# Keeping the FFN activations token-major and taking the F-major copies from transposing DMA loads (SSM block with gated FFN, forward and backward)

## Chip, cores, metric

One core of one Trainium2 chip. The metric is the device time of one execution in microseconds (us), median of several runs. The kernel before took 2763.79 us (3 runs, 2761.97 to 2766.11). "Times in the trace" count from the start of the span.

## The reference

L = 2048 tokens, D = 576 channels, N = 128 states, F = 4608 hidden FFN columns, all bf16. The kernel returns the output and the gradients of all parameters.

```python
xn = _layernorm(x)
s  = ssm(xn, A, B, C, log_dt, Dskip)       # long convolution by FFT
gate = einsum("bsd,df->bsf", xn, w1)
up   = einsum("bsd,df->bsf", xn, w3)
h    = silu(gate) * up
g    = silu(einsum("bsf,fd->bsd", h, w2))
out  = x + s * g                           # and the vjp of all of it with grad_out
```

## The kernel before

The FFN's activations live in DRAM as F-major tiles, [F, tokens]. The backward pass of the FFN has two stages. The *weight stage* goes over 18 groups of 256 F columns; the weight gradients contract over tokens and so need token-major h, gu and gg, which PE makes by transposing F-major tiles through PSUM.

```python
def pe_transpose(self, dst, src):                      # 16 transposes of 128x128
    for g in range(LT // 8):
        pt = self.ps_tr.tile([P, 8, P], BF16, name="ptr6")
        for k in range(8):
            nc.tensor.transpose(pt[:, k, :], src[:, t * P:(t + 1) * P], self.ident_bf[:])
        # evicted by VectorE (g even) or ScalarE (g odd)
...
    nc.vector.memset(go_oT[rem:P, DT - 1, :], 0.0)     # 5th chunk padded to 128 rows
...
    for hh in range(NH):                               # hidden gradient gh, F-major
        ph = ps_h.tile([P, HL], FP32, name="ph")       # HL = 512 tokens
        for c in range(DT):                            # 5 chunks, all of 128 rows
            nc.tensor.matmul(ph[...], lhsT=w2T[:, c, :], rhs=go_oT[:, c, ...],
                             start=(c == 0), stop=(c == DT - 1))
        nc.scalar.copy(out=gh[:, hh * HL:(hh + 1) * HL], in_=ph[:])
```

The *input stage* loads F-major gg and gu for 256 tokens at a time, transposes w1 and w3 by 72 DMA loads, and runs the last GEMM (tile `px`).

Of the kernel before, what the change touches and what calls it, by code (L numbers as in the profile page):

```python
# [11 lines left out]
ALU = mybir.AluOpType  # L12
# [46 lines left out]
class K:  # L59
# [567 lines left out]
    def ffn_scratch(self):  # L627
        cfg = self.cfg
        D, DT, L, LT, FT = cfg.D, cfg.DT, cfg.L, cfg.LT, cfg.FT
        self.TC4 = 256  # L630
        self.G_dram = self.dram.tile([FT, P, L], BF16, name="G_dram")
        self.U_dram = self.dram.tile([FT, P, L], BF16, name="U_dram")
        self.H_dram = self.dram.tile([L // self.TC4, P, FT, self.TC4], BF16, name="H_dram")
        self.GS_dram = self.dram.tile([P, LT, D], BF16, name="GS_dram")
        self.GO_dram = self.dram.tile([P, LT, D], BF16, name="GO_dram")
        self.GOT_dram = self.dram.tile([P, DT, L], BF16, name="GOT_dram")

    def ffn_hidden(self, wp, gup, ps, T0, TA):
# [3 lines left out]
        GRP = 4  # L642
        HL = 1024
        nfull = D // P
        rem = D - nfull * P
        assert FT % GRP == 0 and rem == 64
        xnT = self.xnT
        for fi in range(FT):
            self.at(T0 + TA * fi)
            f0 = fi * P  # L650
            fl = fi % GRP
            if fl == 0:
                wm = {}
                for w in ("B_w1", "B_w3"):
                    wm[w] = wp.tile([P, nfull, GRP * P], BF16, name="wm" + w)
                    nc.sync.dma_start(out=wm[w][:], in_=aps[w][0:nfull * P, f0:f0 + GRP * P].rearrange(
                        "(c p) f -> p c f", p=P))
                wt = wp.tile([P, GRP * P], BF16, name="wtail")
                nc.sync.dma_start(out=wt[0:rem, :], in_=aps["B_w1"][nfull * P:D, f0:f0 + GRP * P])
                nc.sync.dma_start(out=wt[rem:P, :], in_=aps["B_w3"][nfull * P:D, f0:f0 + GRP * P])  # L660
            cs = slice(fl * P, (fl + 1) * P)
            for hh in range(L // HL):
                g_t = gup.tile([P, HL], BF16, name="g_t")
                u_t = gup.tile([P, HL], BF16, name="u_t")
                s_t = gup.tile([P, HL], BF16, name="s_t")
                h_t = gup.tile([P, HL], BF16, name="h_t")
                for q in range(HL // 512):
                    qs = slice(q * 512, (q + 1) * 512)
                    t0 = hh * HL + q * 512
                    pg = ps.tile([P, 512], FP32, name="pg")  # L670
                    pu = ps.tile([P, 512], FP32, name="pu")
                    for (w, pt) in (("B_w1", pg), ("B_w3", pu)):
                        for c in range(nfull):
                            nc.tensor.matmul(pt[:], lhsT=wm[w][:, c, cs], rhs=xnT[:, c, t0:t0 + 512], start=(c == 0),  # L674
                                             stop=False)
                    nc.tensor.matmul(pg[:], lhsT=wt[0:rem, cs], rhs=xnT[0:rem, nfull, t0:t0 + 512], start=False, stop=True)
                    nc.tensor.matmul(pu[:], lhsT=wt[rem:P, cs], rhs=xnT[rem:P, nfull, t0:t0 + 512], start=False, stop=True)
                    nc.scalar.activation(out=s_t[:, qs], in_=pg[:], func=ACT.Silu)
                    if q % 2 == 0:
                        nc.vector.tensor_copy(out=g_t[:, qs], in_=pg[:])  # L680
                    else:
                        nc.scalar.copy(out=g_t[:, qs], in_=pg[:])  # L682
                    nc.scalar.copy(out=u_t[:, qs], in_=pu[:])  # L683
                nc.vector.tensor_tensor(out=h_t[:], in0=s_t[:], in1=u_t[:], op=ALU.mult)
                nch = HL // self.TC4
                nc.sync.dma_start(out=self.H_dram[hh * nch:(hh + 1) * nch, :, fi, :].rearrange("c p l -> p c l"),
                                  in_=h_t[:].rearrange("p (c l) -> p c l", l=self.TC4))
                nc.gpsimd.dma_start(out=self.G_dram[fi, :, hh * HL:(hh + 1) * HL], in_=g_t[:])
                nc.gpsimd.dma_start(out=self.U_dram[fi, :, hh * HL:(hh + 1) * HL], in_=u_t[:])

    def ffn_output(self, T0, TB):
# [3 lines left out]
        TC = self.TC4  # L695
# [5 lines left out]
        with self.tc.tile_pool(name="o_w", bufs=1) as wpool, \  # L701
                self.tc.tile_pool(name="o_h", bufs=3) as hp, \
# [10 lines left out]
            for i in range(LT):  # L713
                self.at(T0 + TB * i)
                k = i % (TC // P)
                if k == 0:
                    hc = hp.tile([P, FT, TC], BF16, name="hc")
                    nc.sync.dma_start(out=hc[:], in_=self.H_dram[i // (TC // P)])
# [7 lines left out]
                for fi in range(FT):  # L726
                    for pi_, (po, pw) in enumerate(pieces):
                        nc.tensor.matmul(po_[:, pi_, 0:pw], lhsT=hc[:, fi, k * P:(k + 1) * P],  # L728
# [247 lines left out]
    def phase6_ffn_bwd(self):  # L976
        nc, cfg = self.nc, self.cfg
        L, FT = cfg.L, cfg.FT
        self.TC6 = 256
        self.GG_dram = self.dram.tile([L // self.TC6, P, FT, self.TC6], BF16, name="GG_dram")  # L980
        self.GU_dram = self.dram.tile([L // self.TC6, P, FT, self.TC6], BF16, name="GU_dram")
        self.phase6_weights()
        self.phase6_inputs()
# [4 lines left out]
    def pe_transpose(self, dst, src):  # L988
        nc, LT = self.nc, self.cfg.LT
        for g in range(LT // 8):  # L990
            pt = self.ps_tr.tile([P, 8, P], BF16, name="ptr6")
            for k in range(8):
                t = g * 8 + k
                nc.tensor.transpose(pt[:, k, :], src[:, t * P:(t + 1) * P], self.ident_bf[:])  # L994
            if g % 2 == 0:
                nc.vector.tensor_copy(out=dst[:, g * 8:(g + 1) * 8, :], in_=pt[:])
            else:
                nc.scalar.copy(out=dst[:, g * 8:(g + 1) * 8, :], in_=pt[:])

    def phase6_weights(self):  # L1000
        nc, cfg = self.nc, self.cfg
        D, DT, L, LT, F, FT = cfg.D, cfg.DT, cfg.L, cfg.LT, cfg.F, cfg.FT
        aps = self.aps
        GRP = 2
        NGRP = FT // GRP
        HL = 512
        NH = L // HL
        pieces = self.dpieces()
        nfull = D // P
        rem = D - nfull * P  # L1010
        assert FT % GRP == 0 and rem == 64
        with self.tc.tile_pool(name="e_big", bufs=1) as big, \
                self.tc.tile_pool(name="e_w", bufs=2) as wp, \
                self.tc.tile_pool(name="e_in", bufs=2) as inp, \
                self.tc.tile_pool(name="e_el", bufs=2) as elp, \
                self.tc.tile_pool(name="e_t", bufs=2) as tp, \
                self.tc.tile_pool(name="e_hn", bufs=3) as hnp, \
                self.tc.tile_pool(name="e_nat", bufs=2) as natp, \
                self.tc.tile_pool(name="e_gw", bufs=2) as gwp, \
                self.tc.tile_pool(name="e_ps_h", bufs=2, space=bass.MemoryType.PSUM) as ps_h, \  # L1020
                self.tc.tile_pool(name="e_ps_tr", bufs=2, space=bass.MemoryType.PSUM) as self.ps_tr, \
                self.tc.tile_pool(name="e_ps_w2", bufs=1, space=bass.MemoryType.PSUM) as ps_w2, \
                self.tc.tile_pool(name="e_ps_gw", bufs=2, space=bass.MemoryType.PSUM) as ps_gw:
            go_o = big.tile([P, LT, D], BF16, name="go_o6")
            go_oT = big.tile([P, DT, L], BF16, name="go_oT6")
            nc.vector.memset(go_oT[rem:P, DT - 1, :], 0.0)
# [3 lines left out]
            for gi in range(NGRP + 1):  # L1030
                if gi < NGRP:
                    tiles = self.phase6_elementwise(gi, GRP, wp, inp, elp, tp, hnp, natp, ps_h, go_oT)
                if gi > 0:
                    self.phase6_weight_grads(gi - 1, GRP, prev, go_o, gwp, ps_w2, ps_gw)
                prev = tiles

    def phase6_elementwise(self, gi, GRP, wp, inp, elp, tp, hnp, natp, ps_h, go_oT):
        nc, cfg = self.nc, self.cfg
        D, DT, L, LT, FT = cfg.D, cfg.DT, cfg.L, cfg.LT, cfg.FT
        aps = self.aps  # L1040
        HL = 512
        NH = L // HL
        gg_n = natp.tile([P, LT, GRP * P], BF16, name="gg_n")
        gu_n = natp.tile([P, LT, GRP * P], BF16, name="gu_n")
        gates, ups, silus, dsls, h_ns = [], [], [], [], []
        for fl in range(GRP):
            fi = gi * GRP + fl
            gate = inp.tile([P, L], BF16, name="gate6")
            nc.gpsimd.dma_start(out=gate[:], in_=self.G_dram[fi])
            gates.append(gate)  # L1050
            silu = elp.tile([P, L], BF16, name="silu6")
            nc.scalar.activation(out=silu[:], in_=gate[:], func=ACT.Silu)
            silus.append(silu)
        for fl in range(GRP):
            dsl = elp.tile([P, L], BF16, name="dsl6")
            self.dsilu(elp, dsl, gates[fl], silus[fl])
            dsls.append(dsl)
        for fl in range(GRP):
            fi = gi * GRP + fl
            up = inp.tile([P, L], BF16, name="up6")  # L1060
            nc.gpsimd.dma_start(out=up[:], in_=self.U_dram[fi])
            hT = elp.tile([P, L], BF16, name="hT6")
# [240 lines left out]
```

## Time and profile before

| stage of the kernel before | from, to (us) | what it is bound by |
|---|---|---|
| SSM forward and first FFN GEMMs | 252, 919 | a chain through PE, DVE and ACT |
| FFN output GEMM (`po`) | 937, 1103 | PE |
| SSM parameter gradients (`pT`) | 1396, 1577 | transposing loads |
| weight stage (`ph`, `pgw`) | 1639, 2391.5 | PE, 41.4 us a group |
| input stage (`px`) | 2391.5, 2759.7 | transposing loads, then PE |

The columns of a timeline are start, length, engine, line, operation, operand, count.

### The profile page before, as it was taken

The numbers are of one execution on the slowest core, as the hardware profiler recorded it, in microseconds if no ns is written. First come the engines' busy times: TensorE is split into PE (matmuls) and PEld (weight loads), VectorE is DVE, ScalarE is ACT, GpSimd is POOL, SyncE is SP. The second block draws the span as 40 slices with busy tenths as digits, with TensorE's granted clock in tenths as the row PEclk, the third lists the DMA queues.
The fourth block names the chain that finished last, engine by engine and source line by source line (L and its number), as shares of the span: only waits on it lengthen the run. The fifth ranks groups of instructions, "written<-read, shape, count | busy, mean of one in ns | idle before, by whom it ended". The sixth has DMA issues, their size and how long they took to land.

```text
span 2759.7 us, 39491 instructions
## 1 busy us (share of the span) xinstructions
PE 2061.2 (75%) x15803; PEld 1342.9 (49%) x15894; DVE 1473.6 (53%) x2361; ACT 1083.3 (39%) x1381; POOL 409.0 (15%) x655
## 2 busy tenths in 40 slices
PE   1797777777899699435343329899999999639999
PEld 0332233223355377324233316676776777527777
DVE  7313767667688355697988964443433444102222
ACT  1357777776755211202000027565565565000000
POOL 1001333333211211000000002222222221100000
PEclk9556787787899899768655559999999999869999
DMA  2245666666764774222299946455454443475441
GB/s 73 91 185 212 238 237 215 222 221 239 260 212 159 261 244 130 78 87 73 64 237 237 230 112 184 143 141 133 144 143 130 142 135 105 96 200 201 163 163 56
DMA packets 479644, 455.14 MB, mean 165 GB/s; under 512 B 266210, under 2 KB 425188, under 8 KB 471652
## 3 DMA queue, kind: packets, MB, share of 16 engines
q1 hardware_dynamic: 338644, 208.82, 27.3%
q10 hardware_dynamic: 106112, 134.65, 14.6%
q0 software_dynamic: 34704, 109.15, 12.0%
q8 instruction: 124, 2.03, 0.3%
q14 instruction: 60, 0.49, 0.1%
HBM read 188.75 MB, written 209.24 MB: 144 GB/s over the span
## 4 chain that ended last, share of the span: by engine, by line
PE 24%; DMA 11%; DVE 10%; issue 7%; SPq 4%; POOL 3%; ACT 0%; POOLq 0%; DVEq 0%; ACTq 0%
PE px L1174 10%; DMA qT<-Q_dram 5%; PE ph L1081 5%; SPq L986 4%; DMA out_dram<-gw 3%; PE pgw L1122 3%; PE pgw L1110 2%; PE ptr L994 1%; DVE cm_t L564 1%; DMA w2T<-w2r 1%; PE et_ps L525 1%; DVE Z L562 1%; DVE cm_t L561 1%; POOL out_dram L1126 1%; DVE Z L565 1%
## 5 line engine op out<-in xcount | busy, mean ns | idle before, releaser
L1174 PE MATMUL px<-w1T,ggc 128*128 128x288 bf16 x1152 | 238.9, 290 | 42.7 <-DMA w1T<-in_B_w_dram 42.7
L1174 PE MATMUL px<-w3T,guc 128*128 128x288 bf16 x1152 | 238.5, 289 | 28.8 <-DMA guc<-GU_dram 18.9
L1122 PEld LDWEIGHTS <-xn_bf 128*128 128x128 bf16 x2304 | 225.8, 98 | 59.6 <-issue 31.6
L674 PEld LDWEIGHTS <-wmB_w 128*128 128x128 bf16 x1152 | 110.1, 103 | 213.7 <-issue 130.6
L1081 PE MATMUL ph<-go_oT,w2T 128*128 128x512 bf16 x682 | 162.5, 382 | 46.0 <-DMA go_oT<-GOT_dram 42.1
L674 PE MATMUL pg<-xnT,wmB_w 128*128 128x512 bf16 x535 | 162.2, 405 | 42.1 <-ACT g_t L682 24.0
L674 PE MATMUL pu<-xnT,wmB_w 128*128 128x512 bf16 x565 | 170.0, 415 | 24.8 <-ACT u_t L683 24.4
L1125 DVE CAST gw<-pgw 128x256 bf16<-128x256 f32 x144 | 60.1, 424 | 229.2 <-DMA out_dram<-gw 139.2
L1178 DVE TENSOR_TENSOR gx<-px,gx 128x288 f32<-128x288 f32 x32 | 13.2, 453 | 294.0 <-PE px L1174 294.0
L728 PE MATMUL po<-w2g,hc 128*128 128x288 bf16 x1152 | 147.7, 290 | 26.3 <-DMA hc<-H_dram 19.7
L1110 PE MATMUL pgw<-go_o,h_n 128*128 128x288 bf16 x1152 | 165.1, 286 | 1.6 <-DMA go_o<-GO_dram 0.7
L886 PE MATMUL pT<-gKK,qT 128*128 128x32 bf16 x1152 | 71.5, 234 | 112.1 <-DMA qT<-Q_dram 108.5
L1122 PE MATMUL pgw<-gg_n,xn_bf 128*128 128x256 bf16 x1152 | 133.6, 276 | 28.3 <-DVE gw L1125 28.3
L1191 ACT ACTIVATE t<-gx 128x576 f32<-128x576 f32 x16 | 10.9, 684 | 365.3 <-DVE gx L1178 365.3
L1174 PEld LDWEIGHTS <-ggc 128*128 128x128 bf16 x1152 | 113.8, 99 | 73.5 <-issue 43.8
L1174 PEld LDWEIGHTS <-guc 128*128 128x128 bf16 x1152 | 113.7, 99 | 60.2 <-DMA guc<-GU_dram 19.5
L728 PEld LDWEIGHTS <-hc 128*128 128x128 bf16 x1152 | 112.9, 99 | 57.5 <-issue 27.0
L1122 PE MATMUL pgw<-gu_n,xn_bf 128*128 128x256 bf16 x1152 | 137.5, 273 | 0.0
L453 POOL COPY pz_k<-p_k 128x512 bf16<-128x512 bf16 x36 | 73.2, 2035 | 433.6 <-DVE p_k L446 433.6
L440 DVE TENSOR_SCALAR m_k<-et_ps 128x512 int32<-128x512 int32 (+1 forms) x180 | 103.4, 625 | 56.3 <-PE et_ps L439 56.3
L1081 PEld LDWEIGHTS <-w2T 128*128 128x128 bf16 x720 | 69.1, 98 | 117.4 <-issue 48.3
L1110 PEld LDWEIGHTS <-h_n 128*128 128x128 bf16 x1152 | 108.8, 98 | 31.2 <-issue 1.0
(319 smaller groups left out, 4396.7 us busy)
## 6 DMA issues: line engine op xcount, KB each, us to landing
Q_dram<-q_k ACTq DMA_DIRECT2D x36, 1024.0 KB, 3.9
E_dram<-E_k SPq DMA_DIRECT2D x36, 576.0 KB, 2.7
E_l<-E_dram SPq DMA_DIRECT2D x36, 576.0 KB, 6.8
G_dram<-g_t POOLq DMA_DIRECT2D x72, 256.0 KB, 4.5
U_dram<-u_t POOLq DMA_DIRECT2D x72, 256.0 KB, 4.7
H_dram<-h_t SPq DMA_DIRECT2D x72, 256.0 KB, 4.8
hc<-H_dram SPq DMA_DIRECT2D x8, 2304.0 KB, 10.9
gate<-G_dram POOLq DMA_DIRECT2D x36, 512.0 KB, 4.5
```

The costliest lines, as they stand in the source:

```text
L440: nc.vector.tensor_scalar(out=m[:, o:o + ow], in0=pt[:, 0:ow].bitcast(I32), scalar1=(1 << 16) - 1, scalar2=None, op0=ALU.bitwise_and)
L453: nc.gpsimd.tensor_copy(out=pz[:, 1:3], in_=p[:].rearrange("p r a d -> p r d a"))
L525: nc.tensor.matmul(pt[:, 0:W], lhsT=mat[:, tt, kt * P:(kt + 1) * P], rhs=src_fn(tt), start=(tt == 0), stop=(tt == KT - 1))
L674: nc.tensor.matmul(pt[:], lhsT=wm[w][:, c, cs], rhs=xnT[:, c, t0:t0 + 512], start=(c == 0), stop=False)
L728: nc.tensor.matmul(po_[:, pi_, 0:pw], lhsT=hc[:, fi, k * P:(k + 1) * P], rhs=w2[fi][:, po:po + pw], start=(fi == 0), stop=(fi == FT - 1))
L886: nc.tensor.matmul(pT[:, dl, k, :], lhsT=qT[:, (1 - k) * DC + dl, :], rhs=gKK[:, :, :, d0 + dl], start=True, stop=True)
L986: self.nc.sync.dma_start_transpose(out=dst, in_=src)
L1081: nc.tensor.matmul(ph[:, q * 512:(q + 1) * 512], lhsT=w2T[:, c, :], rhs=go_oT[:, c, hh * HL + q * 512:hh * HL + (q + 1) * 512], start=(c = ...
L1110: nc.tensor.matmul(pgw[pi_][:, 0:pw], lhsT=h_ns[fl][:, tt, :], rhs=go_o[:, tt, po:po + pw], start=(tt == 0), stop=(tt == LT - 1))
L1122: nc.tensor.matmul(pw_[:, 0:GW], lhsT=self.xn_bf[:, tt, c * P:(c + 1) * P], rhs=nat[:, tt, :], start=(tt == 0), stop=(tt == LT - 1))
L1125: nc.vector.tensor_copy(out=gw[:], in_=pw_[:, 0:GW])
L1174: nc.tensor.matmul(px[pi_][:, 0:pw], lhsT=act[:, fi, k * P:(k + 1) * P], rhs=wT[:, fi, po:po + pw], start=(fi == 0 and ai == 0), stop=(fi ...
```

## The change

All FFN activations are stored token-major. The forward GEMMs swap the roles of their operands, h comes back for the output GEMM through one transposing load per 128 tokens, the weight stage needs no transposes on PE at all, and the input stage gets F-major gg and gu through transposing loads. The core of the diff, with cuts:

```diff
@@ FFN output
-                    nc.sync.dma_start(out=hc[:], in_=self.H_dram[i // (TC // P)])
+                self.nat_transpose(hc[:], self.H_dram[i])
@@ weight stage
-            nc.vector.memset(go_oT[rem:P, DT - 1, :], 0.0)
...
-            self.pe_transpose(h_n[:], hT[:])
-                    nc.tensor.matmul(ph[...], lhsT=w2T[:, c, :], rhs=go_oT[:, c, ...512 tokens],
-            self.pe_transpose(gu_n[...], guT[:])
-            self.pe_transpose(gg_n[...], ggT[:])
+                    for c, (do, dsz) in enumerate(cfg.dch):
+                        nc.tensor.matmul(ph[:, j, :]..., lhsT=go_oT[0:dsz, c, tt * P:(tt + 1) * P],
+                                         rhs=w2T[0:dsz, :, c, :], start=(c == 0), stop=(c == DT - 1))
...
@@ input stage
-                nc.scalar.dma_start(out=ggc[:], in_=self.GG_dram[tc_])
-                nc.scalar.dma_start(out=guc[:], in_=self.GU_dram[tc_])
+                self.nat_transpose(ggc[:], self.GG_dram[i])
+                self.nat_transpose(guc[:], self.GU_dram[i])
```

PSUM is also dealt out anew: `pgw` gets four rotating tiles and `ph` three.

## The prediction

> **What bounds the kernel now.** I read the page of the profile first (busy shares, then the strip of 40 slices), then a table of windows that cuts the span where the program changes stage, then the timeline inside the stages that the change touches.
>
> ```profile
> PE 2061.2 (75%) x15803; PEld 1342.9 (49%) x15894; DVE 1473.6 (53%) x2361; ACT 1083.3 (39%) x1381; POOL 409.0 (15%) x655
> ...
> DMA  2245666666764774222299946455454443475441
> ```
>
> No engine is full over the span: the stages have different limits, so only the windows help. Columns below: window, its length, busy us (and count) of PE, PEld, DVE, ACT and POOL, then granted clock, DMA share, GB/s.
>
> ```profile
> 252.00:925.00 673.00, 542.82 (x3315) 238.59 (x3367) 481.54 (x735) 457.81 (x600) 199.00 (x237) 0.85 0.64 221
> 925.00:1112.00 187.00, 155.95 (x1232) 118.25 (x1232) 89.26 (x136) 23.52 (x49) 22.04 (x41) 0.93 0.64 214
> ...
> 1396.00:1577.00 181.00, 72.47 (x1156) 66.40 (x1155) 162.44 (x209) 0.00 (x0) 0.00 (x0) 0.50 1.13 236
> ```
>
> In order: the SSM forward mixed with the FFN's first GEMMs (PE, DVE and ACT all between 68% and 81% busy: a chain through several engines); the FFN output GEMM (PE); and a stage which the change leaves alone, but which shows the operation that the change adds: 36 transposing loads of the Q scratch keep the DMA share above 1.
>
> ```profile
> 1752.06:2331.24 579.18, 542.58 (x5014) 415.40 (x5040) 233.70 (x322) 339.19 (x364) 136.88 (x272) 1.00 0.47 135
> 2391.50:2486.00 94.50, 22.98 (x149) 15.45 (x148) 0.42 (x1) 0.00 (x0) 1.58 (x3) 0.61 0.72 184
> ```
>
> The first line is the steady part of the FFN backward's weight stage: 14 of its 18 groups, 41.4 us each, PE busy 94% at full clock. PE is the bound there; ACT (59%) and DVE (40%) have room. The second line is the start of the last stage (input gradients): PE is nearly idle while SyncE issues 72 transposing loads of w1 and w3. After it comes the last GEMM, 250.00 us busy in the 250 us from 2490: pure PE.
>
> **What the Trainium skill says, and whether the trace agrees.** "VectorE: DVE Perf Modes", section The three transpose paths, gives a 128x128 bf16 transpose 390 ns on TensorE and 1309 ns by DMA. The trace has 219 ns for one on TensorE, and eight in a row take 0.61 us. By DMA a block costs far less when it is part of a large load: a qT load of 32 blocks takes SyncE 5.33 us, 0.17 us a block. "DMA: Bandwidth & Descriptors", section Latency and other measured facts, gives the DMA transpose 261 GB/s (350 to 400 when contiguous). The trace disagrees: qT loads follow one another every 5.37 us (17 in 91.24 us), 1,048,576 bytes each, so 195 GB/s. "Trainium Kernel Development and Optimization", section Key Constraints, says that DMAs of all queues share 16 DMA engines; the trace agrees, as the share of 1.13 includes the pz loads of another queue. "Perfetto Trace Analysis", section Sequencer Loop, has each engine's sequencer take its instructions one after another; the trace agrees: SyncE's transposes stand in line, and whatever is behind them waits. These are the rows:
>
> ```profile
> L986 SPq DMA_TRANSPOSE qT<-Q_dram x36: 4536/5334/6671, 1381.1 to 1567.2; - x36
> ...
> 1392.43 91.24 SPq L986 DMA_TRANSPOSE qT<-Q_dram  x17
> ...
> L986 SPq DMA_TRANSPOSE w2T<-w2r x36: 1200/1202/2169, 1586.7 to 2302.9; - x36
> ...
> 2403.15 1.26 SPq L986 DMA_TRANSPOSE w1T<-in_B_w_dram  x1
> 2404.46 1.26 SPq L986 DMA_TRANSPOSE w3T<-in_B_w_dram  x1
> ```
>
> **Part 1, the weight stage: what goes.** In each group the parent transposes hT, guT and ggT of two F tiles on PE: 3 x 2 x 16 = 96 transposes, their PSUM evictions on ACT and DVE, and the waits between. All of it goes, because h, gu and gg are now made token-major. From timeline rows such as these
>
> ```profile
> 1988.91 7.15 PE L1122 MATMUL pgw<-gg_n,xn_bf 128*128 128x256 bf16 x64 [1.30 <-DVE gw L1125]
> 1997.86 1.07 PE L994 MATMUL ptr<-ident_bf,hT 128*128 128x128 bf16 x16
> 1960.39 6.85 PE L1081 MATMUL ph<-go_oT,w2T 128*128 128x512 bf16 x31
> ```
>
> a 256-wide matmul is worth about 0.110 us, a transpose about 0.065 us, a 512-wide one about 0.217 us. A group's PE work after the change: gh is 80 matmuls of 256 columns instead of 40 of 512, 80 x 0.110 = 8.8 us; the w2 gradient 64 of 288, at the last stage's pace of 0.1224 us (pairs start 0.245 us apart), 7.8 us; the w1/w3 gradients 128 x 0.110 = 14.1 us; their tail 1.8 us. Sum 32.5 us. I add 0.9 us for the short waits at new PSUM tiles: 33.4 us. Before it was 41.4 us: 32.4 us of the same GEMMs, 96 x 0.065 = 6.2 us of transposes, and 2.8 us of waits. The biggest wait was for the eviction of a gradient tile (24.3 us in these 14 groups), since DVE had only two PSUM tiles to empty there. The change lets four tiles rotate, so PE can run ahead while each output DMA frees its buffer about 4.0 us after the cast began. Saved: 18 x 8.0 = 144 us. Filling the stage may cost more than it did, because Silu is now one instruction for a whole group and gates the first gh evictions: 5 us back. Net -139.
>
> ACT does not take over. Per group, two activations of 4096 columns (twice 1.91 us each, so 7.6), two table loads (2.6), eight gh evictions (8 x 0.587 = 4.7), four of gw2 (1.7), and eight DMA issues (about 3): 19.6 of 33.4 us. DVE: 16 products of 1024 columns at 0.69 plus nine casts at 0.42: 14.8 us.
>
> **Part 2, the input stage.** The parent's gg and gu loads were plain DMAs on ACT's queue; PE started on them while the weight transposes were arriving. Now they are transposes on SyncE, behind all 72 of w1 and w3 (this is how the built program stands). The built program also makes the first w1 transpose wait for the very last matmul of the weight stage; in the parent it waited for the last w2-gradient matmul, and started at 2375.8, 15.7 us before PE ended the stage at 2391.5. So after PE ends: 72 x 1.308 = 94.2 us; then the first gg tile, 36 blocks. The line through w2T (5 blocks, 1.20 us) and qT (32 blocks, 5.33 us) gives 0.153 us a block, so 36 blocks take 5.9 us. The gu tile takes another 5.9 us, and landing follows issue by some 3 us: PE starts 109 us after the stage before ends. From there 16 tiles x 144 matmuls x 0.1224 = 282 us, 2 us for the cold clock, and the same 7.2 us tail: 400 us. Before: 2759.7 - 2391.5 = 368 us. So +32; I say +34, for some disturbance.
>
> Later tiles are hidden: two transposes are 11.8 us of DMA, and the tile's rest (0.58 MB) about 1.6 us, against 17.6 us of PE.
>
> **Part 3, the FFN output stage.** Each 128-token tile now needs one transposing load of 36 blocks, 5.9 us, where half of a plain load stood (2,359,296 bytes landing in 10.9 us for two tiles). PE needs about 9 us a tile. Other traffic, about 1 MB a tile, is 2.6 to 3.2 us at the 320 to 400 GB/s that plain loads reach. So 8.5 to 9.1 of DMA against 9 of PE: close to even. +5 us.
>
> **Part 4, the first GEMMs.** The operands swap roles: 1440 matmuls of 512 columns as before, and the same evictions. G and U go out as 288 DMAs of 128 KB instead of 144 of 256 KB. At about 0.6 us each POOL gains some 93 us, but it is 30% busy in this stage. H goes out in runs of 1 KB instead of 512 B. I count 0, and 12 us either way for another interleaving.
>
> Sum: 2763.8 - 139 + 34 + 5 = 2664 us, 3.6% less.
>
> **The rivals.** (a) Hidden anyway: the weight stage's transposes fill PE's waits for evictions, and their removal brings only the waits forward. For it: DVE waited 139 us for output DMAs there, and two output buffers at 4.0 us allow one gradient tile in 2.0 us, while PE makes one in 1.76. Against it: nine tiles lag by about 2 us in all, and the stage ends with PE on other work for 17 us. If it held, a group would take 38 us and the total 2664 + 18 x 4.6 = 2747. (b) The DMA engines become the bound wherever transposes came in. For it: 195 GB/s and a share above 1 in the Q stage. If a transpose of 36 blocks took 9 us with other traffic beside it, the output stage would take 12 us a tile (+45) and the input stage 20 (+38): about 2745. Against it: qT ran at 5.37 us with pz beside it. (c) Better than thought: if the transposes of w1 and w3 ran faster with no plain loads mixed in, or the waits of the weight stage vanished altogether (32.5 us a group), 2664 - 16 - 10 = 2638.
>
> **Range and chances.** The weight stage's gain carries the sign; its error is about 1 us a group, 18 us. The input stage's start is off by 10 us at most, as its parts are measured; output and first stage 10 to 15 us each. Together about 28 us, with a longer tail upwards for (a) and (b): 2632 to 2708. The line for faster by 2% lies at 2708.5. Faster 0.88, same 0.11, slower 0.01.
>
> **What would show it.** Right: no ptr matmuls from hT, guT and ggT; groups of gh 33 to 34 us apart; PE idle about 109 us before px, ended by a gu transpose; then px without gaps; SyncE transposes of hc, ggc and guc near 5.9 us. Wrong: groups at 36 us or more with waits for gw; transposes of 36 blocks well over 7 us; waits of po or px for hc, ggc or guc after the first tile; a first GEMM stage more than 12 us from its 673 us.

## More of the kernel before

Note D = 4 x 128 + 64: every contraction over D has four full chunks of 128 rows and one of 64.

```profile
1960.33 5.55 PEld L1081 LDWEIGHTS <-w2T 128*128 128x128 bf16 x27
```

27 weight loads of the hidden gradient (the loads of a matmul's lhsT) follow one another and no wait is recorded ahead of them: each is made while an earlier matmul runs.

## The result

The changed kernel took 2719.36 us (median of 4 runs, 2717.45 to 2723.87), beside 2764.95 us for the kernel before (4 runs). The ratio is 0.9837, 95% interval 0.9819 to 0.9854: faster, but by less than 2%. A ratio here is the mean time of one kernel's fast runs over that of the other's of the same rounds, so not quite the ratio of the medians quoted. The prediction of 2664 us is 55 us too low, and 2719 lies outside its range.

The page of the profile after, busy time first, then the DMA strip over 40 slices:

```profile
PE 2024.5 (74%) x14886; PEld 1289.5 (47%) x14886; DVE 1418.1 (52%) x2396; ACT 929.7 (34%) x1203; POOL 519.0 (19%) x763
...
DMA  3245656666665798323179947655555552488873
```

In the strip the output stage (14th to 16th digit) went from 7 7 4 to 7 9 8, and the end, from 4 7 5 4 4 1 to 4 8 8 8 7 3: there stand the new transposing loads.

The table of windows of the kernel after, with the columns explained in the prediction:

```profile
252.00:925.00 673.00, 559.01 (x3367) 237.51 (x3367) 483.87 (x735) 456.90 (x600) 322.95 (x374) 0.86 0.63 219
925.00:1112.00 187.00, 154.36 (x1232) 117.81 (x1232) 87.89 (x131) 22.95 (x48) 27.41 (x48) 0.92 0.90 219
...
1752.00:2290.00 538.00, 538.00 (x4562) 401.99 (x4561) 200.21 (x370) 224.21 (x236) 128.84 (x257) 1.00 0.52 152
```

The last line is the surprise: in the steady weight stage PE is busy 538.00 of 538.00 us. There are no waits left to remove, and yet a group is longer than worked out. The timeline of PE in one group (the tail's rows are left out) tells which part:

```profile
1971.90 11.93 PE L1038 MATMUL ph<-w2T,go_oT 128*128 128x256 bf16 x78
1983.77 8.01 PE L1061 MATMUL pgw<-go_o,h_n 128*128 128x288 bf16 x64
...
1991.84 7.15 PE L1072 MATMUL pgw<-gu_n,xn_bf 128*128 128x256 bf16 x64
1998.82 7.15 PE L1072 MATMUL pgw<-gg_n,xn_bf 128*128 128x256 bf16 x64
2007.77 0.39 PE L1038 MATMUL ph<-w2T,go_oT 128*128 128x256 bf16 x2
```

The next group starts 2007.77 - 1971.90 = 35.87 us later (its row shows two matmuls only because the window ends there). The weight-gradient rows cost what was predicted: 64 matmuls of 256 columns in 7.0 us, 0.109 each. The hidden gradient does not: 78 matmuls of the same 256 columns take 11.93 us, 0.153 each. The timeline of the weight loads at that point:

```profile
1971.92 0.10 PEld L1038 LDWEIGHTS <-go_oT 128*128 128x128 bf16 x1
1972.22 0.55 PEld L1038 LDWEIGHTS <-go_oT 64*128 64x128 bf16 x5 [0.21 <-issue]
1972.98 0.55 PEld L1038 LDWEIGHTS <-go_oT 64*128 64x128 bf16 x5 [0.21 <-issue]
```

The unbroken run of the kernel before is cut into pieces of five. A merged row carries the shape of its first load: each piece is one load of 64 rows and the four of 128 rows after it, and ahead of each piece there are 0.21 us without a weight load. A token tile takes 0.755 us, where five matmuls of 0.109 would be 0.545.

That points to a part of the diff that I had read past: the line that goes, `memset(go_oT[rem:P, ...])`, was the zero padding of the fifth chunk. The parent multiplied 128 rows, half of them zeros; the change multiplies the 64 rows with data.

Where the time of the two profiles went, from the first and last matmuls of each stage (times in the trace; the column "padded" is the first experiment):

| event | before | after | padded |
|---|---|---|---|
| last `po` (FFN output) starts | 1102.9 | 1105.6 | 1105.0 |
| last `pT` (parameter gradients) starts | 1576.8 | 1584.6 | 1586.5 |
| first `ph` (weight stage) starts | 1639.3 | 1649.2 | 1649.9 |
| PE ends the weight stage | 2391.5 | 2318.4 | 2262.4 |
| span | 2759.7 | 2717.6 | 2662.2 |

So the weight stage, from its first `ph`, went from 752.2 to 669.2 us, -83; the input stage from 368.2 to 399.2, +31; and the start of the weight stage came 9.9 us later, of which 2.7 had arisen by the end of the output GEMM, 5.1 in the parameter gradients, which the change leaves alone, and 2.1 in what follows. Together -83 + 31 + 10 = -42, as the spans say.

### The profile page after: what moved, and what is told of

It reads as the page before. It is cut to its first block, busy times and chain, and to the rows that moved or that the text cites. A ratio compares the mean times of both kernels' runs of the same rounds, so it can differ in the third digit from the quotient of the medians.

```text
span 2717.6 us, 37783 instructions
## 1 busy us (share of the span) xinstructions
PE 2024.5 (74%) x14886; PEld 1289.5 (47%) x14886; DVE 1418.1 (52%) x2396; ACT 929.7 (34%) x1203; POOL 519.0 (19%) x763
## 4 chain that ended last, share of the span: by engine, by line
PE 37%; DVE 9%; DMA 8%; SPq 4%; issue 1%; ACT 0%; POOL 0%; ACTq 0%; DVEq 0%; POOLq 0%
PE px L1116 10%; PE pgw L1072 9%; PE ph L1038 8%; DMA qT<-Q_dram 6%; PE pgw L1061 5%; SPq L977 4%; DVE cm_t L564 1%; PE et_ps L525 1%; PE pgw L1079 1%; DVE Z L562 1%; PE inv_ps L541 1%; DVE cm_t L561 1%; DVE Z L565 1%; DVE Z L566 1%; PE pT L879 1%
## 5 line engine op out<-in xcount | busy, mean ns | idle before, releaser
L1116 PE MATMUL px<-w1T,ggc 128*128 128x288 bf16 x1152 | 236.5, 287 | 103.3 <-DMA ggc<-GG_dram 103.3
L1038 PE MATMUL ph<-w2T,go_oT 128*128 128x256 bf16 (+1 forms) x1440 | 228.9, 282 | 54.8 <-issue 40.4
L671 PE MATMUL pg<-wmB_w,xnT 128*128 128x512 bf16 x576 | 178.7, 432 | 68.8 <-ACT g_t L678 44.5
L671 PEld LDWEIGHTS <-xnT 128*128 128x128 bf16 x1152 | 112.0, 105 | 234.0 <-issue 161.4
L1038 PEld LDWEIGHTS <-go_oT 128*128 128x128 bf16 (+1 forms) x1440 | 117.6, 98 | 164.3 <-issue 117.9
L671 PE MATMUL pu<-wmB_w,xnT 128*128 128x512 bf16 x576 | 180.7, 430 | 2.0 <-ACT u_t L679 2.0
L1040 ACT CAST gh<-ph 128x512 bf16<-128x512 f32 x144 | 80.5, 586 | 257.1 <-PE ph L1038 252.4
L721 PE MATMUL po<-w2g,hc 128*128 128x288 bf16 x1152 | 146.0, 289 | 27.1 <-DMA hc<-H_dram 27.1
L879 PE MATMUL pT<-gKK,qT 128*128 128x32 bf16 x1152 | 71.7, 233 | 116.6 <-DMA qT<-Q_dram 113.6
L1061 PE MATMUL pgw<-go_o,h_n 128*128 128x288 bf16 x1152 | 145.0, 287 | 0.0
L1017 POOL MEMSET w2r<- 128x64 bf16 x36 | 5.7, 158 | 722.8 <-PE pT L879 501.8
L685 POOL DMA_DIRECT2D G_dram<-g_t x144 | 106.1, 737 | 165.9 <-ACT g_t L678 160.9
L1041 DVE TENSOR_TENSOR gu_n<-gh,gu_n 128x1024 bf16<-128x1024 bf16 x72 | 49.7, 690 | 154.9 <-ACT gh L1040 154.9
```

The source lines that it names most:

```text
L671: nc.tensor.matmul(pt[:], lhsT=xnT[:, c, ts], rhs=wm[w][:, c, :], start=(c == 0), stop=False)
L685: nc.gpsimd.dma_start(out=dst[fb * (FB // self.FG) + k, :, i0:i0 + NT, :], in_=src[:, :, gs])
L721: nc.tensor.matmul(po_[:, pi_, 0:pw], lhsT=hc[:, fi, :], rhs=w2[fi][:, po:po + pw], start=(fi == 0), stop=(fi == FT - 1))
L879: nc.tensor.matmul(pT[:, dl, k, :], lhsT=qT[:, (1 - k) * DC + dl, :], rhs=gKK[:, :, :, d0 + dl], start=True, stop=True)
L1038: nc.tensor.matmul(ph[:, j, :].rearrange("p (a f) -> p a f", f=P), lhsT=go_oT[0:dsz, c, tt * P:(tt + 1) * P], rhs=w2T[0:dsz, :, c, :], sta ...
L1040: nc.scalar.copy(out=gh[:, t2 * 2:t2 * 2 + 2, :], in_=ph[:])
```

## The experiments

The theory (A): a change of row count inside a run of matmuls, 128 to 64 and back, stops the weight loads from running ahead and costs PE about 0.21 us, 16 times a group. The rivals: (A2) the 64-row matmul itself is slow; (B) the new operand form, an rhs in two blocks of 128 columns with go_oT as weights, is slow at any row count; (C) another engine holds the group.

### 1. The changed kernel, padded to 128 rows again

```diff
+            nc.vector.memset(go_oT[rem:P, DT - 1, :], 0.0)
-  lhsT=go_oT[0:dsz, c, tt * P:(tt + 1) * P], rhs=w2T[0:dsz, :, c, :]
+  lhsT=go_oT[:, c, tt * P:(tt + 1) * P],     rhs=w2T[:, :, c, :]
```

> The changed kernel with one thing of the old one put back: the fifth chunk of 64 rows is padded with zeros to 128 rows, so that all five matmuls of a hidden-gradient tile use all 128 rows. Same count of matmuls, same 256 columns. Theory A (each change between 128-row and 64-row weights stops the weight loads from running ahead and costs about 0.21 us, 16 times a group): the 78 recorded hidden-gradient matmuls of a group fall from 11.9 to about 8.6 us, the group from 35.9 to about 32.5 us, and the kernel from 2719 to about 2660 us. Rival B (the rhs in two blocks of 128 columns, or the new order with go_oT as weights, makes 256-column matmuls slow whatever the rows): no change, 2719 us within 5. Rival C (something other than PE sets the group once PE is faster): the matmuls get shorter but the group stays above 34 us, 2690 us or more.

Measured: 2666.29 us (2660.99 to 2671.53), ratio to before 0.9644 (0.9618 to 0.9671). PE's timeline of a group, then the weight loads in it:

```profile
1913.40 8.69 PE L1039 MATMUL ph<-w2T,go_oT 128*128 128x256 bf16 x78
...
1945.92 4.32 PE L1039 MATMUL ph<-w2T,go_oT 128*128 128x256 bf16 x38
```

```profile
1913.96 2.06 PEld L1039 LDWEIGHTS <-go_oT 128*128 128x128 bf16 x19
```

The same 78 matmuls, now with more zeros to multiply, take 8.69 us, and a group 1945.92 - 1913.40 = 32.52 us. The weight loads run unbroken again. B falls, since the operand form is the same as in the changed kernel; C falls, since the group shrank with PE's work alone, by 3.35 us. The weight stage is 612.5 us, 56.7 less than in the changed kernel.

### 2. The kernel before, with the 64 rows only

```diff
-  lhsT=w2T[:, c, :],                           rhs=go_oT[:, c, ...]
+  lhsT=w2T[0:(P if c < DT - 1 else rem), c, :], rhs=go_oT[0:(P if c < DT - 1 else rem), c, ...]
```

> The kernel before with the one thing of the change that I had overlooked: the fifth chunk of its hidden-gradient matmuls uses only its 64 rows that hold data, in place of 128 padded ones. There are 8 such 512-column runs in a group, so half of the excursions that the changed kernel has. Theory A: 8 times 0.21 us is 1.7 us more PE time a group, 18 groups; the old group has PE waits for evictions that can hide part, so 10 to 31 us slower, 2775 to 2796 us. Rival B: the cost belongs to the two-block rhs or the new operand order, which are not here: no change, 2765 us within 4.

Measured: 2792.49 us (2790.51 to 2799.83) beside 2767.06 us, ratio 1.0103 (1.0081 to 1.0125): 1% slower, which is 28 us. The groups of weight loads by shape in a window of the steady stage (busy us, mean ns, then the idle time ahead of them and its cause):

```profile
L1082 PEld LDWEIGHTS <-w2T 128*128 128x128 bf16 x352 | 28.6, 98 | 33.7 <-issue 14.9
L1082 PEld LDWEIGHTS <-w2T 64*128 64x128 bf16 x87 | 8.0, 92 | 35.1 <-issue 35.1
```

The cost arises in the old operand form too, ahead of the 64-row loads, at half the number of places and about half the size: 28 us over 8 x 18 excursions is 0.19 us each. Multiplying fewer rows made the parent slower.

### 3. The changed kernel with the chunks in snake order

```diff
+                    order = list(enumerate(cfg.dch))
+                    if tt % 2:
+                        order = order[::-1]
-                        ... start=(c == 0), stop=(c == DT - 1))
+                        ... start=(n == 0), stop=(n == DT - 1))      # n: place in the order
```

> The changed kernel with the chunks taken 0 to 4 in even token tiles and 4 to 0 in odd ones, so that two 64-row matmuls stand next to each other and the number of excursions to 64 rows is halved, 8 a group in place of 16, with the same number of 64-row matmuls. Theory A (cost per change of row count): 8 times 0.21 us saved a group, group 35.9 to about 34.2 us, kernel about 2689 us. Rival A2 (cost per 64-row matmul, such as a slower load of 64 rows): no change, 2719 us. Rival B (two-block rhs): no change.

Measured: 2691.03 us (2688.01 to 2694.95), ratio 0.9732 (0.9713 to 0.9751); against the 0.9837 of the changed kernel that is 1.05% of 2765 us, 29 us less. The timeline of PE for the 78 matmuls, and of the weight loads:

```profile
1924.84 10.36 PE L1041 MATMUL ph<-w2T,go_oT 128*128 128x256 bf16 x78
```

```profile
1925.16 0.11 PEld L1041 LDWEIGHTS <-go_oT 64*128 64x128 bf16 x2 [0.21 <-issue]
1925.48 0.77 PEld L1041 LDWEIGHTS <-go_oT 128*128 128x128 bf16 x8 [0.21 <-issue]
1926.46 0.11 PEld L1041 LDWEIGHTS <-go_oT 64*128 64x128 bf16 x2 [0.21 <-issue]
```

As many 64-row matmuls as before, but now in pairs, with no gap inside a pair. Here the gap of 0.21 us stands on both sides of the 64-row loads, while the changed kernel showed it ahead of them only; gaps of weight loads can lie under running matmuls, so the cost is better read from the matmuls. With 16, 8 and 0 excursions to 64 rows, the same 78 matmuls take 11.93, 10.36 and 8.69 us: (11.93 - 8.69) / 16 = 0.20 us and (10.36 - 8.69) / 8 = 0.21 us for each excursion. The cost belongs to the change of row count, not to the 64-row matmul: A2 falls as well.

### 4. Room for the first loads of the weight stage

The weight stage also fills more slowly than I had allowed. The changed kernel's load of the first gates waits 50.6 us; its buffer lies, by the order of the pools, on memory that the parameter gradients still use. I moved all buffers of the stage up by an unused tile.

```diff
+        with self.tc.tile_pool(name="e_pad", bufs=1) as padp, \
+            pad = padp.tile([P, FT, D], BF16, name="pad")       # 41,472 bytes a partition
```

> The changed kernel with an unused tile of 41 KB a partition ahead of the weight stage's buffers, so that the buffers for the gate and hidden activations of the first groups no longer lie on memory that the parameter-gradient stage still uses; nothing else changes. Theory: the 16 us that the filling of the weight stage costs more than in the kernel before come from these loads waiting for the last small stores of the parameter gradients (50.6 us of wait on that load). With the loads earlier I expect 5 to 15 us less, about 2709 us. Rival: the filling waits for the transposed output gradient, whose loads wait as well, and now all the more because its buffer moves onto that memory: no change or some us worse, 2715 to 2725 us. Nothing here should change the steady group of 35.9 us.

Measured: 2709.88 us (2708.05 to 2711.81), ratio 0.9799 (0.9781 to 0.9817). The size fits, the reason does not. The first gates are loaded at 1592.3 us in place of 1649.4, as meant, but the first `ph` came at 1676.3 us, 27 later than in the changed kernel. Now the loads of both copies of the output gradient are late: they are issued at 1656.5 to 1660.6 us, in the changed kernel at 1631.2 to 1648.2. PE's recorded wait, 53.4 us, is for the token-major copy, at four weight-gradient matmuls that the built program had put first. That these two tiles now lay on the busy memory is read from the layout; no run moves them alone. The stage ended at 2325.2, 6.8 us later. The gain arose in the input stage. The waits of PE there, first of the changed kernel, then of this one (total us, times, longest):

```profile
PE px L1116 <- DMA ggc<-GG_dram: 103.3, 1, 103.3
PE px L1116 <- DMA guc<-GU_dram: 4.6, 1, 4.6
```

```profile
PE px L1119 <- DMA ggc<-GG_dram: 88.5, 1, 88.5
PE px L1119 <- DMA guc<-GU_dram: 5.1, 1, 5.1
```

With the shift the first weight transpose starts at 2309.3 us, 15.9 us before PE ends the stage. SyncE's recorded wait ahead of it now ends with the last w2-gradient matmul, where it had ended with the stage's very last one. The likely reason, by the sizes of the tiles, is that w3T no longer lies on the gate buffers; that is argued, not shown.

### 5. The first loads again, with a layout that frees all of them

```diff
-                self.dma(go_oT[0:dsz, c, :], self.GOT_dram[0:dsz, c, :])
+                nc.gpsimd.dma_start(out=go_oT[0:dsz, c, :], in_=self.GOT_dram[0:dsz, c, :])
# and the pools reordered, so that only late-used tiles lie on the parameter gradients' memory
```

> The changed kernel with the weight stage's buffers laid out so that the transposed output gradient, and the gate and hidden activations of the first groups, lie on no memory that the end of the parameter-gradient stage uses, and with the transposed output gradient loaded over GpSimd's queue, which is idle there, and not behind the small stores of that stage. Nothing of the steady groups changes. Theory: what delays the filling of the weight stage is the load of the transposed output gradient (issued at 1631 to 1648 us in the trace, landing 19 us later), as the shifted run suggests, whose first hidden-gradient matmul came 27 us later, when that load did. I expect the first such matmul at about 1615 us in place of 1649 and the weight stage to end 15 to 30 us earlier than at 2318 us; the kernel at 2675 to 2700 us (some 14 us of it in the last stage, as in the shifted run, if its weight loads start earlier again). Rival: VectorE is busy with the parameter gradients until about 1637 us and its products hold the hidden gradients' evictions back, so the weight stage ends at most 8 us earlier.

Measured: 2711.81 us (2706.41 to 2714.98), ratio 0.9801 (0.9778 to 0.9825). The first `ph` came at 1623.4 us, 26 us earlier, but the stage ended at 2303.6, only 14.8 us earlier: PE then waited 25.9 us for the other, token-major copy of the output gradient, which I had left on the busy memory (its load is issued at 1654.4 us). The last stage did not gain here, as the first gu transpose stayed behind the weights in the queue. So the filling was worth about 15 us in the profiled run, the fastest of the four; the medians differ by 7.6 us. The stage is at the low end of what I expected, and the kernel missed its 2675 to 2700 us, which had counted on 14 us from the last stage as well.

### 6. w1's transposes ahead of the last stage

The tile that was unused in run 4 now holds transposed w1, loaded during the weight stage.

```diff
+            self.w1T = w1p.tile([P, cfg.FT, cfg.D], BF16, name="w1T")     # pool opened before the stage
+                    for fi in range(2 * gi, 2 * gi + 2):
+                        self.nat_transpose(self.w1T[:, fi:fi + 1, :], self.aps["B_w1"][:, fi * P:(fi + 1) * P])
```

> The layout of the shifted run, with its unused tile now put to use: it holds the transposed first weight, which the last stage needs, and its 36 transposing loads are issued during the weight stage instead of after it. Theory: the 103 us that the input stage waits at its start are 72 weight transposes of 1.264 us in one queue and then the first two activation transposes of 5 us each; with 36 of them gone from the path, 45 us go, and the others may start some 15 us before the weight stage ends, when the buffers they overlie come free. From 2710 us (the shifted run) I expect 2645 to 2665 us, and the wait ahead of the first input-gradient matmul to fall from 89 to about 40 us. Rival: the transposes in the weight stage crowd out that stage's own loads and stores, and the group of 35.9 us grows: the sum stays above 2690 us.

Measured: 2688.48 us (2685.99 to 2691.79), ratio 0.9719 (0.9693 to 0.9744). Both theories had a part. The wait ahead of `px` fell from 88.5 to 41.5 us, but the weight stage ended at 2350.5 us, 25.3 later than in run 4. The order of issue had been left to the program's scheduler, and it bunched the 36 loads. SyncE's queue, then ACT's evictions of `ph`:

```profile
1685.07 2.58 SPq L979 DMA_TRANSPOSE w2T<-w2r  x2
1687.70 21.10 SPq L979 DMA_TRANSPOSE w1T<-in_B_w_dram  x15
1708.96 2.90 SPq L979 DMA_TRANSPOSE w2T<-w2r  x2
```

```profile
1713.30 1.56 ACT L1044 CAST gh<-ph 128x512 bf16<-128x512 f32 x3 [15.05 <-DMA w2T<-w2r]
1720.51 1.07 ACT L1044 CAST gh<-ph 128x512 bf16<-128x512 f32 x2 [5.65 <-DMA w1T<-in_B_w_dram]
```

By the recorded releasers, ACT's waits ahead of these evictions end with transposing loads. ACT issues its stores of gu and gg in between, and takes its instructions in order: the last store before the 15.05 us wait ends is issued at 1712.82 us, and the eviction follows at 1713.30. So I read that the stores wait for the transposing loads, the evictions behind the stores, and PE with them (12.7 us at `ph` for `gh`; none in run 4).

### 7. The same, spread over the groups

```diff
+  nc.vector.tensor_copy(out=self.w1T[:, 2 * gi:2 * gi + 2, 0:1], in_=tiles[1][:, 0:2, 0:1])   # then the two transposes
```

> The first weight's transposes moved into the weight stage, spread the same way, alone on the changed kernel with the shifted layout (64-row chunks as changed). Theory: the shifted run at 2710 us loses only the 47 us of wait that the unspread run took out of the start of the last stage, and pays nothing for it in the weight stage: 2660 to 2668 us. Rival (DMA engine time): 2685 us or more, as unspread.

Measured: 2663.90 us (2656.52 to 2665.66), ratio 0.9625 (0.9603 to 0.9646). The weight stage ends at 2323.6 us, in run 4 at 2325.2, and the wait stays at 41.2 us. Two transposes a group cost the stage nothing; the row of 36 did.

### 8 and 9. All mends together

Padding, a free layout (arranged a little otherwise than in run 5) and w1 early, first with the bunched transposes and then spread. The source of both also places w3's transposes after the loads of the first gg and gu tiles; in the trace of the last kernel the scheduler still issued 35 of the 36 ahead of them, from 2247.2 us.

> All three mends together, as a kernel to beat both: the chunk of 64 rows padded to 128, the loads for the weight stage's beginning early, and the first weight's transposes for the last stage done during the weight stage. If the parts add up: 2666 us (padded alone) less about 20 us of filling less about 60 us in the last stage, so 2575 to 2600 us. If one mend only moves the wait to another engine or to the DMA engines, 2620 us or more.

Measured: 2627.11 us (2626.61 to 2630.37), ratio 0.950 (0.948 to 0.952), the slower of the two expectations.

> The three mends again, with the first weight's transposes now spread over the groups, two after each (each pair waits for a one-column copy out of that group's gradients, which the transpose then overwrites). In the run with all three, these 36 stood in a row at 1662 to 1716 us in one queue and kept the weight of the third group waiting behind them. Theory: that row cost the weight stage about 35 us (it ended at 2291 us where the padded kernel, starting later, ended at 2262), so the kernel goes from 2627 to 2590 to 2600 us. Rival: the transposes cost the weight stage the same wherever they stand, because they take DMA engine time from its loads and stores: no change, 2620 to 2630 us.

Measured: 2597.45 us (2595.07 to 2603.18), ratio 0.9387 (0.9367 to 0.9407), correct. Spreading gave 30 us, as expected, though by way of ACT rather than of the third group's weight that the expectation names: PE's waits at `ph` for `gh` fell from 28.8 to 0.2 us. This kernel is 6.1% faster than the one before and beats the changed one by 0.9387 / 0.9837, 4.6%.

## Why the prediction was wrong

**The step that failed.** "gh is 80 matmuls of 256 columns instead of 40 of 512, 80 x 0.110 = 8.8 us." In the trace it is 12.1 us (11.87 to the first `pgw`, and two matmuls that stand later, 0.22). I took 0.110 us from matmuls that all use 128 rows, and treated row count as free. Each token tile has one 64-row chunk, and each excursion to it costs 0.20 us: 16 x 0.20 = 3.2 us a group, 18 groups, 58 us. Padding removes 56.7 us from the weight stage and brings the kernel to 2666 us, 2 us from the predicted 2664. The diff showed the cause, the removed memset and the `0:dsz` slices, and I had not asked what they cost.

The warning could have been found, first of all in the trace of the kernel before. Its first GEMMs have 64-row chunks too, and they stand in a window that I had printed before predicting:

```profile
402.34 1.03 PE L674 MATMUL pu<-xnT,wmB_w 128*128 128x512 bf16 x4
403.30 0.09 PEld L677 LDWEIGHTS <-wtail 64*128 64x128 bf16 x1 [0.42 <-issue]
403.30 0.39 PE L677 MATMUL pu<-xnT,wtail 64*128 64x512 bf16 x1
403.62 1.04 PE L674 MATMUL pg<-xnT,wmB_w 128*128 128x512 bf16 x4
```

From 402.34 to 403.62 five matmuls of 512 columns take 1.28 us, where five of 0.217 would be 1.085: 0.20 us more, the same excursion. Both kernels have 288 such 64-row matmuls in that stage; no run pads them, so what they cost there is open.

The Trainium skill, "TensorEngine Tiling (Array Packing)", section Key Properties, says: "Changing tiling mode (not just tile) drains the TensorE". I had not looked it up, since nothing in the diff is called tiling; a 64-row operand in a run of 128-row ones behaves like such a change, and the runs put 0.20 us on it. Two more signs fit: in the kernel before, a 64-row matmul on the lower half of the rows and one on the upper half start together, at 405.45 and 405.46 us; and in the changed kernel the tail's 64-column weight loads, at 1970.03 us, and the 128-column ones after them, at 1971.90, have gaps of 0.21 and 0.20 us ahead of them too. "TensorE: Matmul & The Clock Gate", section Step-by-step: what each phase is for, describes how PE pulls weight loads ahead of running matmuls; the kernel before shows it in unbroken runs (27 loads in 5.55 us), and the changed kernel shows it interrupted at each 64-row load. Whether the array drains or the load is only held back, these traces cannot tell; either could leave the 0.21 us gap.

**The other steps of part 1.** The w2 gradient (7.8 us), the w1/w3 gradients (14.1) and the tail (1.8) came out at 7.85, 14.06 and 1.87. The 0.9 us for waits at new PSUM tiles was not needed: PE was busy all the time, and the padded group is 32.52 us, the bare sum. Filling cost more than the 5 us put down: the stage's length beyond 18 steady groups was 752.2 - 18 x 41.4 = 7 us before, 669.2 - 18 x 35.87 = 23.5 after, so 16.5 us. The reason that I gave, evictions held back, has 8.9 us of recorded waits of PE; 5.5 us more are waits for the transposed output gradient. In the padded kernel the two misses cancel: its groups save the 18 x 0.9 = 16 us that I had put down for waits, and its filling, 612.5 - 18 x 32.52 = 27 us, costs 20 more than before, 15 above my 5. So 612.5 is 139.7 less than 752.2, against -139 predicted. Part of the closeness of 2666 to 2664 is therefore luck. That ACT and DVE would not take over was right.

**Part 2** was right: +34 predicted, +31 measured, PE idle 103.3 + 4.6 us against 109. The transposing loads of gg took SyncE 4.60 us in the median and those of gu 5.87, where I had 5.9 for both. The later tiles were hidden, as `px` ran without gaps.

**Parts 3 and 4** were right within their error: +5 and 0 predicted, +2.7 together. The DMA share of the output stage rose from 0.64 to 0.90, so it was close, but PE waited for `hc` only once, 27.1 us at the start. The transposing loads of hc took SyncE 5.00 us in the median, not 5.9. POOL gained 124 us in the first stage, not 93, and hid it. The 5.1 us lost in the parameter gradients were in no step. PE's waits for the qT loads grew there by as much, from 108.5 to 113.6 us; why these loads came later stays unexplained.

**The rivals.** (a), the gain hidden by eviction waits with groups of 38 us, did not happen: waits at `pgw` vanished. By length alone the group of 35.87 us lies between my 33.4 and its 38; it is PE's busy time that rules it out. (b), DMA as the bound, did not happen in either stage. None of the rivals was the one that came true, a matmul that is slower by its shape in the middle of others; the range had no room for it.

## What to carry to other kernels

When a contraction leaves a remainder of 64 rows in a run of 128-row matmuls, padding it with zeros can be faster than multiplying fewer rows; if it can't be padded, put remainders next to each other. In a diff, ask of every slice that changes a matmul's rows or columns what it does to the instructions before and after it, and price a matmul only from rows with the same neighbours. Where buffers of a new stage lie on memory of an old one, read which of its first loads wait, and spread loads that are moved ahead, since a row of them blocks whatever waits behind it.

## What the Trainium skill lacked or had wrong

- "TensorEngine Tiling (Array Packing)", Key Properties: the drain at a change of tiling mode has no figure, and the page does not say that a plain 64-row chunk in a 128-row accumulation meets it. The runs show 0.20 to 0.21 us for each excursion to 64 rows (11.93, 10.36 and 8.69 us for 16, 8 and 0 of them), 1 to 2% of this kernel.
- "TensorE: Matmul & The Clock Gate", Step-by-step: what each phase is for: the conditions under which a weight load is pulled ahead are given in row groups and a background buffer; what a load of 64 rows among loads of 128 does is not said. The runs show a gap of 0.21 us ahead of a 64-row load after 128-row ones, and none between two 64-row loads.
- "VectorE: DVE Perf Modes", The three transpose paths: 1309 ns for a 128x128 transpose by DMA is not what a block costs in a large load. For loads of 36 blocks SyncE took 4.60 us (gg) and 5.87 us (gu) in the median, 0.13 and 0.16 us a block; no run has one block alone.
- "DMA: Bandwidth & Descriptors", Latency and other measured facts: 261 GB/s for the DMA transpose, 350 to 400 when contiguous. Over the median time that SyncE took, a gg load of 1,179,648 bytes in 4.60 us is 256 GB/s and a gu load in 5.87 us is 201; qT ran at 195. All lie below the lower figure.
- No page says what a row of transposing loads does to another engine: with 36 of them bunched in SyncE's queue, ACT's evictions waited (and its stores, as I read it) and the weight stage lost 25.3 us; two a group cost nothing that shows.
